# First tile of an attention kernel with two gated layers: low part of a weight unit issued inside the gate, first state pair split before the softmax

## The chip, the cores and the metric

The kernel runs on one core of one Trainium2 chip. The metric is the device time of one execution in microseconds (us), the median of three runs. The engines are TensorE (PE in the profile: matrix products; PEld: its weight loads), VectorE (DVE), ScalarE (ACT), GpSimd (POOL) and SyncE (SP). Each engine works through its own instructions in program order and waits at the head of its queue for semaphores. DMAs are issued from the queues of SP, ACT and POOL.

## The reference

```python
B, H, S, Ns, D = 8, 8, 512, 32, 64
scores  = x @ state.T / sqrt(D);  a  = softmax(scores)    # per batch and head
xread   = a @ state                                        # 512 rows per batch
scores2 = state @ x.T / sqrt(D);  a2 = softmax(scores2)
sread   = a2 @ x                                           # 32 rows per batch
x = concat(xread, sread) -> [4352, 512]                    # 8 * (512 + 32) tokens
h = x @ w_in1;  x = (h * sigmoid(1.702 * h)) @ w_out1      # 512 -> 2048 -> 512
h = x @ w_in2;  out = (h * cos(h)) @ w_out2
```

The weights arrive as 64-bit floating-point numbers, all else as float32.

## The kernel before

**Precision.** Every matrix product of the two layers is made of three products of halves: each operand is split into a high part (rounded to fp32r by a ScalarE copy) and a low part (VectorE: the value minus its high part), and high by high, high by low and low by high are summed in PSUM.

**Weights.** One layer's weights are cut into 16 units of 1 MB, named i0 to i7 (input side) and o0 to o7 (output side); a unit serves two chunks of 128 hidden features. Units are fetched in the order i0, i1, o0, i2, o1, i3, o2, ..., i7, o6, o7 (`seq`). The 64-bit words are decoded in the first tile's steps, each unit in five passes of 128x1024 elements. `decode_begin` (line 107) makes two ScalarE passes, `top` (line 120, into one of two buffers `u`) and `bottom` (line 123, in place on the raw words); `decode_end` (line 127) makes `bits` (VectorE, line 136, joins the two), `hi` (ScalarE, line 142) and `lo` (VectorE, line 146). A unit is begun in one step and ended in the next.

**Steps.** Tokens are worked in 9 tiles (8 batches of 512 rows and a tail of 256 rows), the hidden features in 16 chunks. The main loop (line 612) has one step for each layer m, tile t and chunk c. A step issues, in this order: `hidden` (chunk c of h, 12 products of 512 columns for the first tile), `second` of the chunk two steps back (12 products into the four `py` accumulators; its results free that chunk's `gh` and `gl`), the `gate` of chunk c, DMA fetches, `split_state` or `load_pair` where due, attention pieces of the next batch (`run_piece`), `sw_piece`s, and last the `lo()` that `gate` returned.

`gate` (line 376) issues on ScalarE: tanh (382), `top` of the next unit, `gh` (372), `bottom` of the next unit, `hi` of the unit begun a step earlier; and on VectorE: line 384 (the gate's product), `bits` (136), `gl` (374). In step c of the first tile the unit ended is seq[c + 1]: in odd steps c = 1, 3, ..., 13 it is o0 to o6, first needed by `second` in step c + 1, behind step c + 1's `hidden`; in even steps it is an input unit, first needed by `hidden` of step c + 2 (for i1, step 2).

**Attention in the first tile.** The pieces of batch 1 run in tile 0: the first halves of the heads in steps 1 to 8, the second halves in steps 8 to 15. On VectorE the larger ones are `max_n` and `max_s` (steps 2 and 9), `norm_s` (4, 11), `norm_n` (5, 11), `place_s` (9, 15). Their PSUM tiles (`psA`, `psB`, `psC`) come from a pool of two buffers, `psa`.

**State times input weights.** For tiles 1 to 7 the input product is folded: `sw_piece` (line 167) multiplies the split states of a pair of batches (`rhi`, `rlo`) by the input weights into a `psS` tile, from the same pool `psa`; ScalarE copies its high part (179), VectorE makes the low part (180), and GpSimd issues its store to DRAM (183). Pair 0's pieces are issued in steps 2, 4, 5, 6, 7, 7, 10, 11, 11, 12, 13, 13 and 15 of tile 0 and the next ones in tile 1. The tables `sw_steps` and `todo_split` (lines 516 and 526) set these steps by hand: pair 0 is split in step 1 of tile 0, pair 1 in step 7 of tile 1, and three steps after a split the next pair is loaded into the same `rblk`.

**Prologue.** Lines 557 to 598: batch 0's attention on the token side, with unit i0 decoded between its passes. The state of batch 0 is loaded into `rblk` from ScalarE's queue, used by `xread`, and then `load_pair(0)` follows into the same buffer from SP's queue. The whole schedule is written by hand (`manual_schedule`).

Of the kernel before, what the change touches and what calls it, by code (L numbers as in the profile page):

```python
# [10 lines left out]
F32 = mybir.dt.float32  # L11
# [3 lines left out]
AF = mybir.ActivationFunctionType  # L15
ALU = mybir.AluOpType
# [4 lines left out]
B, H, S, NS, D = 8, 8, 512, 32, 64  # L21
DM, DFF = 512, 2048
P = 128
KD = DM // P
# [17 lines left out]
def attention_two_mlps(  # L42
# [12 lines left out]
    nc = tc.nc  # L55
# [6 lines left out]
    op = ctx.enter_context(tc.tile_pool(name="op", bufs=2))  # L62
# [7 lines left out]
    PAIRS = ((1, 2), (3, 4), (5, 6), (7,))  # L70
# [8 lines left out]
    rblk = const.tile([P, KD, P], F32, name="rblk")  # L79
    rhi = const.tile([P, KD, P], F32R, name="rhi")  # L80
    rlo = const.tile([P, KD, P], F32R, name="rlo")
# [8 lines left out]
    def fetch_w(m, nm, j):  # L90

        src = {"i": (w_in1, w_in2), "o": (w_out1, w_out2)}[nm][m]
        raw = wp.tile([P, UNIT, 2], I32, name=f"raw{nm}{m}_{j}", tag=f"w{nm}{j}")
        for e in range(2):
            words = src[2 * j + e].bitcast(I32)
            if nm == "i":
                nc.sync.dma_start(
                    out=raw.rearrange("p (k e f) w -> p k e (f w)", k=KD, e=2)[:, :, e, :],
                    in_=words.rearrange("p (k f) -> p k f", k=KD),
                )  # L100
            else:
                nc.sync.dma_start(out=raw.rearrange("p (e d) w -> p e (d w)", e=2)[:, e, :], in_=words)
        rawt[m, nm, j] = raw
# [91 lines left out]
    at = ctx.enter_context(tc.tile_pool(name="at", bufs=1))  # L195
# [6 lines left out]
    def load_state(b, queue=nc.sync):  # L202
        queue.dma_start(out=rblk.rearrange("p k d -> p (k d)"), in_=st[b])

    def load_pair(p):

        for i in range(2):
            nc.sync.dma_start(
                out=rblk[:, :, i * D:(i + 1) * D], in_=stT[(*PAIRS[p], 0)[i]].rearrange("p (k c) -> p k c", k=KD)
            )  # L210

    def split_state():
        nc.scalar.activation(out=rhi, in_=rblk, func=AF.Copy)
        nc.vector.tensor_tensor(out=rlo, in0=rblk, in1=rhi.bitcast(F32), op=ALU.subtract)

    def load_xT(b, g, tags=("xT0", "xT1")):
        for j in range(2):
# [158 lines left out]
    def gate(t, c, stores, unit):  # L376

        bits, hi, lo = decode_end()
        top, bottom = decode_begin(*unit) if unit else (lambda: None,) * 2
        ph = ht.pop((0, t, c))  # L380
        t1 = ep.tile([P, sizes[t]], F32, name="t1", tag="t1")
        nc.scalar.activation(out=t1, in_=ph, func=AF.Tanh, scale=0.5 * GATE)  # L382
        g = t1
        nc.vector.scalar_tensor_tensor(out=g, in0=t1, scalar=1.0, in1=ph, op0=ALU.add, op1=ALU.mult)  # L384
        bits()
        for s in stores[:1]:
            s()
        if not stores:
            top()
        low = split_g(0, t, c, g)  # L390
        for s in stores[1:]:
            s()
        if stores:
            top()
        bottom()
        hi()
        low()
        return lo

    def cosine(t, c, stores, before, unit, end):  # L400

# [89 lines left out]
    def warm(n):  # L491

        ps = ps_y.tile([P, P], F32, name="idle", tag="py3")
        for _ in range(n):
            nc.tensor.matmul(ps, ident, ident, start=True, stop=True)
# [30 lines left out]
    todo_split = {step: p for p, (step, _) in enumerate(sw_steps)}  # L526
# [28 lines left out]
    with tc.manual_schedule():  # L555
        seq = [("i", 0), ("i", 1)] + [(nm, j + 2 * (nm == "i")) for j in range(KF // 2) for nm in "oi" if nm == "o" or j + 2 < KF // 2]
        load_xT(0, 0)
        load_state_t(0, nc.scalar)
        load_xT(0, 1, ("a20", "a21"))
        load_state(0, nc.scalar)  # L560
        fetch_w(0, *seq[0])
        make_identity(nc, ident)
        nc.vector.memset(half_pi, math.pi / 2.0)
        first = [
            attn_pieces(0, 0, ((ps_h, "ph"), (ps_h, "ph"))),
            attn_pieces(0, 1, ((ps_y, "py0"), (ps_y, "py1")), "a2T", "a21"),
        ]
        new_x(("x", 0), S)
        warm(3)
        first[0]["scores"]()  # L570
        first[1]["scores"]()
        fetch_w(0, *seq[1])
        load_xT(1, 0)
        load_state_t(1)
        for u in seq[2:5]:
            fetch_w(0, *u)

        def do(*names):
            for name in names:
                first[int(name[-1])][name[:-2]]()  # L580

        do("max_n 0", "exp_n 0")
        for part in decode_begin(0, *seq[0]):
            part()
        do("max_n 1", "exp_n 1", "sum_n 0", "turn_n 0")
        warm(22)
        load_xN(1, 0)
        do("xread 0")
        bits, hi, lo = decode_end()
        bits()  # L590
        hi()
        do("sum_n 1", "turn_n 1", "split_x 0")
        lo()
        do("xread 1")
        load_pair(0)
        for part in decode_begin(0, *seq[1]):
            part()
        do("split_x 1")

        steps1 = [(0, t, c) for t in (*range(B - 1), B, B - 1) for c in range(KF)]  # L600
        steps2 = [(1, t, c) for t in (*range(B // 2), B, *range(B // 2, B)) for c in range(KF)]
        steps = steps1 + steps2
        order = [t for _, t, c in steps if c == 0]


        fetches = {(0, 0, c): (0, *u) for c, u in enumerate(seq[5:])}
        units = {(0, 0, c): (0, *u) for c, u in enumerate(seq[2:])}
        fetches.update({steps1[steps1.index((0, B, 0)) + 2 * j + 2]: (1, "i", j) for j in range(KF // 2)})
        fetches.update({steps[steps.index((0, B - 1, 0)) + 2 * j + 3]: (1, "o", j) for j in range(KF // 2)})
        at2 = [(0, B, c) for c in (6, 9, 12, 15)] + [(0, B - 1, c) for c in range(2, KF, 2)] + [(1, 0, c) for c in (3, 5, 7, 10, 12)]  # L610
        units.update({at_: (1, nm, j) for at_, (nm, j) in zip(at2, ((nm, j) for nm in "io" for j in range(KF // 2)))})
        for i, (m, t, c) in enumerate(steps):
            if m == 0 and c == 0 and t + 1 < B:
                new_x(("a", t + 1), S, range(2))
                plan(i, t)
            if i + 1 < len(steps):
                hidden(m, t, c)
            if i + 2 == len(steps):
                hidden(*steps[-1])
            stores = second(*steps[i - LAG]) if i >= LAG else []  # L620
            unit = units.get((m, t, c))
            if m == 0:
                lo = gate(t, c, stores, unit)
            else:
                lo = cosine(t, c, stores, steps[i - 1][1:] if steps[i - 1][0] == 1 else None, unit, i + 1 == len(steps))
            if (m, t, c) in fetches:
                fetch_w(*fetches[m, t, c])
            if m == 0 and (t, c) in todo_split:
                split_state()
            if m == 0 and (t, c - 3) in todo_split and todo_split[t, c - 3] + 1 < len(PAIRS):  # L630
                load_pair(todo_split[t, c - 3] + 1)
            for b, name in todo.pop(i, ()):
                run_piece(b, int(name[-1]), name[:-2])
            for piece in todo_sw.get((t, c), ()) if m == 0 else ():
                sw_piece(*piece)
            lo()
            if m == 0:
                if t == 0 and c in (9, 11, 13, 14):
                    load_sw(1, (c - 8) // 2)
                if t == 0 and c == KF - 1:  # L640
                    for j in range(4, 8):
                        load_sw(1, j)
                if t == 1 and c < 4 or 1 < t < B and c + 8 < KF:
                    load_sw(t, c + 8)
                if t == 1 and 7 <= c < 11:
                    load_sw(t, c + 5)
                if 0 < t < B - 1 and c >= 8:
                    load_sw(t + 1, c - 8)
            if m == 0 and t == B - 2 and c == KF - 2:
                split_tail()  # L650
            j = i // KF
            if j + 1 < len(order) and i + KF >= len(steps1):
                if c == 2:
                    load_y(order[j + 1])
                if c in (7, 9, 11, 13):
                    split_y(order[j + 1], (c - 7) // 2, nc.gpsimd if m else nc.vector)
        times(*steps[-1][1:])()
        for s in steps[len(steps) - LAG:]:
            for w in second(*s):
                w()  # L660
# [43 lines left out]
```

## Time and profile before

| what | value |
|---|---|
| median of three runs (lowest, highest) | 1492.33 us (1488.96, 1492.51) |
| the profiled execution's own time | 1492.88 us |
| its span | 1491.1 us |
| TensorE busy in the span | 1455.3 us, 98% |
| VectorE, ScalarE, GpSimd busy | 927.7, 646.7, 111.4 us |
| mean granted clock of TensorE | 0.994 |

The span is what the profiler covers; the execution's own time is 1.8 us longer. A busy engine is one that has an instruction under way; TensorE's products are pipelined, so that a product of 512 columns lasts 0.39 us in a row while one starts every 0.23 us. In a row of the timeline the first number is the start, the second the length, and the bracket at the end says how long the engine had been idle before it and what released it. The name `py` is the second product's accumulator, `ph` the hidden one's, `wo` and `wi` are units, `swo` a folded piece.

### The profile page before, as it was taken

How to read it: one execution, taken by the hardware profiler on the slowest of the kernel's cores; microseconds unless marked ns; L12 is line 12 of the kernel's file. 1: busy time of each engine (PE TensorE's matmuls, PEld its weight loads, DVE VectorE, ACT ScalarE, POOL GpSimd, SP SyncE). 2: the span in 40 equal slices, each digit the busy share in tenths (PEclk: the TensorE clock that was granted, in tenths of full speed). 3: DMA queues.
4: the chain of work that ended last, by engine and by line, in shares of the span. 5: the costliest groups of instructions: out<-in, count | busy, mean ns of one | idle time of the engine just before them, and what ended most of it. 6: DMA issues, size and time to landing. Idle time of an engine off the chain costs nothing.

```text
span 1491.1 us, 19321 instructions
## 1 busy us (share of the span) xinstructions
PE 1455.3 (98%) x7306; PEld 1192.2 (80%) x7306; DVE 927.7 (62%) x1642; ACT 646.7 (43%) x1078; POOL 111.4 (7%) x155
## 2 busy tenths in 40 slices
PE   7979999999999999999999999999999999999998
PEld 4767778788888888898887888888888888888886
DVE  6765565556464646456678666666677666666665
ACT  5754434343434343466655333333344333333433
POOL 0111011101111000100001010000000000101000
PEclk9999999999999999999999999999999999999999
DMA  9655566565656453466400101000011001010000
GB/s 346 204 152 152 159 171 171 156 172 138 169 144 165 107 145 91 124 195 205 136 34 1 57 1 57 0 14 30 0 58 43 0 10 48 0 57 1 29 1 29
DMA packets 81340, 140.58 MB, mean 94 GB/s; under 512 B 11616, under 2 KB 38368, under 8 KB 81248
## 3 DMA queue, kind: packets, MB, share of 16 engines
q1 hardware_dynamic: 72000, 109.60, 23.4%
q0 software_dynamic: 8960, 29.37, 8.1%
q8 instruction: 57, 0.93, 0.3%
q10 hardware_dynamic: 288, 0.39, 0.1%
q14 instruction: 35, 0.29, 0.1%
HBM read 92.14 MB, written 47.19 MB: 93 GB/s over the span
## 4 chain that ended last, share of the span: by engine, by line
PE 81%; DVE 7%; ACT 3%; DMA 1%; issue 1%; POOL 0%; ACTq 0%; DVEq 0%
PE py L450 43%; PE ph L365 23%; PE ph L358 10%; PE psS L175 2%; PE psC L318 1%; DMA out<-o 1%; PE psA L234 1%; DVE r L411 1%; DVE r L416 1%; DVE d L415 1%; DVE gl L374 1%; DVE wo L146 1%; ACT gh L372 0%; ACT o L457 0%; DVE u L136 0%
## 5 line engine op out<-in xcount | busy, mean ns | idle before, releaser
L365 PE MATMUL ph<-xh,wi 128*128 128x512 f32 (+1 forms) x1280 | 404.0, 379 | 0.6 <-ACT wi L142 0.5
L450 PE MATMUL py<-gh,wo 128*128 128x512 f32 (+1 forms) x1152 | 367.0, 382 | 14.7 <-DVE wo L146 12.7
L450 PE MATMUL py<-wo,gh 128*128 128x512 f32 x1088 | 336.4, 390 | 1.0 <-ACT gh L372 0.7
L365 PEld LDWEIGHTS ph<-xh,wi 128*128 128x128 f32 x1280 | 237.2, 188 | 49.4 <-ACT wi L142 1.4
L450 PEld LDWEIGHTS py<-gh,wo 128*128 128x128 f32 x1152 | 215.0, 190 | 59.9 <-DVE wo L146 15.7
L365 PE MATMUL ph<-xl,wi 128*128 128x512 f32 (+1 forms) x640 | 241.0, 379 | 0.0
L450 PEld LDWEIGHTS py<-wo,gh 128*128 128x128 f32 x1088 | 202.8, 188 | 44.1 <-ACT o L457 2.3
L450 PE MATMUL py<-gl,wo 128*128 128x512 f32 (+1 forms) x576 | 219.1, 380 | 0.0
L450 PE MATMUL py<-wo,gl 128*128 128x512 f32 x544 | 213.0, 391 | 4.8 <-DVE gl L374 4.5
L374 DVE TENSOR_TENSOR gl<-t,gh 128x512 fp32r<-128x512 f32 (+1 forms) x144 | 97.4, 677 | 177.7 <-ACT gh L372 177.5
L418 ACT ACTIVATE r<-r,half_pi 128x512 f32<-128x512 f32 (+1 forms) x144 | 101.0, 701 | 245.5 <-DVE r L417 245.5
L372 ACT ACTIVATE gh<-t 128x512 fp32r<-128x512 f32 (+1 forms) x144 | 87.5, 608 | 256.8 <-PE py L450 160.3
L411 DVE TENSOR_SCALAR r<-r 128x512 f32<-128x512 f32 (+1 forms) x144 | 65.5, 455 | 180.2 <-ACT r L407 179.8
L358 PE MATMUL ph<-xh,swt 128*128 128x512 f32 x448 | 160.8, 399 | 0.0
L407 ACT ACTIVATE r<-ph 128x512 f32<-128x512 f32 (+1 forms) x144 | 82.3, 572 | 169.3 <-PE ph L365 169.3
L384 DVE SCALAR_TENSOR_TENSOR t<-t,ph 128x512 f32<-128x512 f32 (+1 forms) x144 | 94.1, 653 | 85.0 <-ACT t L382 84.7
L365 PEld LDWEIGHTS ph<-xl,wi 128*128 128x128 f32 x640 | 120.3, 188 | 22.9 <-DVE xl L286 0.2
L450 PEld LDWEIGHTS py<-wo,gl 128*128 128x128 f32 x544 | 102.1, 188 | 30.5 <-DVE gl L374 9.5
L450 PEld LDWEIGHTS py<-gl,wo 128*128 128x128 f32 x576 | 109.4, 190 | 20.4
L431 DVE TENSOR_TENSOR r<-r,ph 128x512 f32<-128x512 f32 (+1 forms) x144 | 94.6, 657 | 46.4 <-ACT r L418 46.4
L382 ACT ACTIVATE t<-ph 128x512 f32<-128x512 f32 (+1 forms) x144 | 82.0, 570 | 87.1 <-PE ph L358 68.7
L358 PEld LDWEIGHTS ph<-xh,swt 128*128 128x128 f32 x448 | 84.8, 189 | 28.5 <-issue 11.9
(76 smaller groups left out, 1490.6 us busy)
## 6 DMA issues: line engine op xcount, KB each, us to landing
sd<-swo POOLq DMA_DIRECT2D x112, 256.0 KB, 3.6
swt<-sd SPq DMA_DIRECT2D x112, 256.0 KB, 4.0
rawi<-in_w_in SPq DMA_DIRECT2D x32, 512.0 KB, 6.9
rawo<-in_w_out SPq DMA_DIRECT2D x32, 512.0 KB, 6.0
xT_t<-in_xT SPq DMA_DIRECT2D x36, 256.0 KB, 4.2
xN_t<-in_xN SPq DMA_DIRECT2D x16, 512.0 KB, 3.7
yd<-o SPq DMA_DIRECT2D x32, 256.0 KB, 3.3
yraw<-yd SPq DMA_DIRECT2D x32, 256.0 KB, 4.4
```

What stands on the lines that cost most here:

```text
L175: nc.tensor.matmul(out_, l[:, k, :], r[:, sl], start=(e == 0 and i == 0), stop=(e == 1 and i == 2), skip_group_check=True)
L358: nc.tensor.matmul(ph, l, r, start=(g == 0 and i == 0), stop=(g == 1 and i == 2))
L365: nc.tensor.matmul(ph, w[:, f0:f0 + P], x, start=(w is wh and k == 0 and x is xk[0][0]), stop=(w is wl and k == KD - 1))
L372: nc.scalar.activation(out=gh, in_=g, func=AF.Copy)
L374: return lambda: nc.vector.tensor_tensor(out=gl, in0=g, in1=gh.bitcast(F32), op=ALU.subtract)
L382: nc.scalar.activation(out=t1, in_=ph, func=AF.Tanh, scale=0.5 * GATE)
L384: nc.vector.scalar_tensor_tensor(out=g, in0=t1, scalar=1.0, in1=ph, op0=ALU.add, op1=ALU.mult)
L407: nc.scalar.activation(out=r, in_=ph, func=AF.Copy, scale=1.0 / (2.0 * math.pi), bias=0.25)
L411: nc.vector.tensor_scalar(out=r, in0=r, scalar1=MAGIC, scalar2=MAGIC, op0=ALU.add, op1=ALU.subtract)
L418: nc.scalar.activation(out=r, in_=r, func=AF.Sin, bias=half_pi)
L431: nc.vector.tensor_tensor(out=r, in0=r, in1=ph, op=ALU.mult)
L450: nc.tensor.matmul(yt[k], l, r, start=(c == 0 and i == 0), stop=(c == KF - 1 and i == 2))
```

## The change

In `gate`, `hi` is issued before `bottom` on ScalarE, and `lo` is issued at once behind `gl` on VectorE instead of at the end of the step; `gate` then returns an empty function. This holds for every gate of the first layer that ends a unit; `cosine` is as before. The first state pair is loaded in the prologue from ScalarE's queue into a buffer of its own (`pair0`, in the place of tag `xN`) and split ahead of the softmax, its low part on GpSimd; the split in step 1 and the load in step 4 go, and the load that stood behind `xread` brings pair 1. Two more warm-up products are issued before the scores.

```diff
-    def load_pair(p):
+    def load_pair(p, into=rblk, queue=nc.sync):
         for i in range(2):
-            nc.sync.dma_start(
-                out=rblk[:, :, i * D:(i + 1) * D], in_=stT[...]
+            queue.dma_start(
+                out=into[:, :, i * D:(i + 1) * D], in_=stT[...]
             )
-    def split_state():
-        nc.scalar.activation(out=rhi, in_=rblk, func=AF.Copy)
-        nc.vector.tensor_tensor(out=rlo, in0=rblk, in1=rhi.bitcast(F32), op=ALU.subtract)
+    def split_state(src=rblk, engine=nc.vector):
+        nc.scalar.activation(out=rhi, in_=src, func=AF.Copy)
+        engine.tensor_tensor(out=rlo, in0=src, in1=rhi.bitcast(F32), op=ALU.subtract)
...
+        hi()
         bottom()
-        hi()
         low()
-        return lo
+        lo()
+        return lambda: None
...
         load_state(0, nc.scalar)
+        pair0 = at.tile([P, KD, P], F32, name="pair0", tag="xN")
+        load_pair(0, pair0, nc.scalar)
         fetch_w(0, *seq[0])
...
-        warm(3)
+        warm(5)
...
+        split_state(pair0, nc.gpsimd)
         do("max_n 0", "exp_n 0")
...
-        load_pair(0)
+        load_pair(1)
...
-            if m == 0 and (t, c) in todo_split:
+            if m == 0 and todo_split.get((t, c), 0):
                 split_state()
-            if m == 0 and (t, c - 3) in todo_split and todo_split[t, c - 3] + 1 < len(PAIRS):
+            if m == 0 and todo_split.get((t, c - 3), 0) and todo_split[t, c - 3] + 1 < len(PAIRS):
                 load_pair(todo_split[t, c - 3] + 1)
```

## Rows read from the trace of the kernel before

**Rows 1.** The page, part 1: busy us, share of the span, instructions of TensorE.
```profile
PE 1455.3 (98%) x7306; PEld 1192.2 (80%) x7306; DVE 927.7 (62%) x1642; ACT 646.7 (43%) x1078; POOL 111.4 (7%) x155
```

**Rows 2.** Waits of TensorE, 0 to 140 us: us in total, times, longest.
```profile
PE py L450 <- DVE wo L146: 12.7, 7, 3.4
```

**Rows 3.** Windows of 12 us: length; busy us of PE, PEld, DVE, ACT, POOL; PEclk; DMA; GB/s.
```profile
28.00:40.00 12.00, 8.78 (x34) 6.65 (x33) 7.18 (x9) 7.74 (x11) 0.00 (x0) 0.86 1.06 377
88.00:100.00 12.00, 8.84 (x34) 6.65 (x33) 8.51 (x18) 5.72 (x7) 0.00 (x0) 0.86 0.49 169
108.00:120.00 12.00, 8.55 (x31) 6.78 (x30) 6.45 (x10) 5.49 (x9) 2.39 (x4) 0.72 0.36 89
```

**Rows 4.** Timeline around steps 1 and 2, several engines: start, length, instruction.
```profile
29.95 1.05 ACT L142 ACTIVATE wo<-u 128x1024 fp32r<-128x1024 f32 x1
...
31.06 0.50 PE L450 MATMUL py<-gh,wo 128*128 128x512 f32 x1 [1.57 <-ACT wo L142]
...
31.56 0.69 DVE L214 TENSOR_TENSOR rlo<-rblk,rhi 128x512 fp32r<-128x512 f32 x1 [1.78 <-ACT rhi L213]
32.17 1.22 DVE L146 TENSOR_TENSOR wo<-u,wo 128x1024 fp32r<-128x1024 f32 x1
...
33.44 1.22 PE L450 MATMUL py<-gh,wo 128*128 128x512 f32 x2 [1.65 <-DVE wo L146]
...
37.44 0.63 ACT L372 ACTIVATE gh<-t 128x512 fp32r<-128x512 f32 x1 [2.80 <-PE py L450]
```

**Rows 5.** Timeline of step 11 and the start of step 12.
```profile
103.91 0.68 DVE L384 SCALAR_TENSOR_TENSOR t<-t,ph 128x512 f32<-128x512 f32 x1
...
104.50 1.22 DVE L136 SCALAR_TENSOR_TENSOR u<-u,rawo 128x1024 int32<-128x1024 int32 x1
...
105.64 1.13 ACT L123 ACTIVATE rawi<-rawi 128x1024 int32<-128x1024 uint32 x1
...
106.39 0.15 DVE L301 TENSOR_SCALAR s<-s 128x1 f32<-128x1 f32 x1
...
106.67 1.06 ACT L142 ACTIVATE wo<-u 128x1024 fp32r<-128x1024 f32 x1
...
109.75 1.25 DVE L180 TENSOR_TENSOR swo<-psS,swo 128x512 fp32r<-128x512 f32 x2
...
110.92 1.20 DVE L146 TENSOR_TENSOR wo<-u,wo 128x1024 fp32r<-128x1024 f32 x1
...
112.18 1.22 PE L450 MATMUL py<-gh,wo 128*128 128x512 f32 x2 [3.45 <-DVE wo L146]
```

**Rows 6.** Timeline of VectorE in step 9.
```profile
88.50 1.79 DVE L329 STREAM_TRANSPOSE xs<-psC 32x32 f32<-32x32 f32 x8
...
92.51 1.22 DVE L146 TENSOR_TENSOR wo<-u,wo 128x1024 fp32r<-128x1024 f32 x1
```

**Rows 7.** Timeline of TensorE, second product of step 13 to that of step 14.
```profile
121.33 0.39 PE L450 MATMUL py<-gh,wo 128*128 128x512 f32 x1
...
124.05 0.40 PE L175 MATMUL psS<-wi,rhi 128*128 128x256 f32 x2
...
129.86 0.74 PE L450 MATMUL py<-gh,wo 128*128 128x512 f32 x2 [1.02 <-DVE wo L146]
...
132.39 0.86 PE L318 MATMUL psC<-xN_t,a2T 128*32 128x128 f32 x24
```

**Rows 8.** Timeline of the prologue, several engines.
```profile
9.44 0.63 ACT L249 ACTIVATE T<-T 128x512 f32<-128x512 f32 x1 [6.49 <-DVE T L248]
...
10.90 1.05 POOL L248 TENSOR_TENSOR T<-T,m 128x512 f32<-128x512 f32 x1 [9.59 <-DVE m L244]
...
11.38 0.59 DVE L259 TENSOR_SCALAR s<-s 128x16 f32<-128x16 f32 x1
...
15.47 0.17 DVE L259 TENSOR_SCALAR s<-s 128x16 f32<-128x16 f32 x1
```

**Rows 9.** Line 208, the pair's loads: us from issue to landing.
```profile
DMA to landing us min/median/max: 3.3/5.5/9.9
```

More of the change, by code (lines that the diff above doesn't have):

```diff
@@ L203, in load_state @@
         queue.dma_start(out=rblk.rearrange("p k d -> p (k d)"), in_=st[b])
-    def load_pair(p):
+    def load_pair(p, into=rblk, queue=nc.sync):
         for i in range(2):
-            nc.sync.dma_start(
-                out=rblk[:, :, i * D:(i + 1) * D], in_=stT[(*PAIRS[p], 0)[i]].rearrange("p (k c) -> p k c", k=KD)
-            )
-    def split_state():
-        nc.scalar.activation(out=rhi, in_=rblk, func=AF.Copy)
-        nc.vector.tensor_tensor(out=rlo, in0=rblk, in1=rhi.bitcast(F32), op=ALU.subtract)
+            queue.dma_start(
+                out=into[:, :, i * D:(i + 1) * D], in_=stT[(*PAIRS[p], 0)[i]].rearrange("p (k c) -> p k c", k=KD)
+            )
+    def split_state(src=rblk, engine=nc.vector):
+        nc.scalar.activation(out=rhi, in_=src, func=AF.Copy)
+        engine.tensor_tensor(out=rlo, in0=src, in1=rhi.bitcast(F32), op=ALU.subtract)
     def load_xT(b, g, tags=("xT0", "xT1")):
```

## The prediction

> **What bounds the kernel now.** The page comes first: TensorE is busy 98% of the span [rows 1], so 36 us of the span lie between its products, and an edit of the order can win only idle time and time at the lower clock. The table of who waited for whom says where: from 0 to 140 us TensorE waits seven times, 12.7 us in total, for VectorE's low part of an output unit (line 146) [rows 2]. These are the odd steps 1, 3, ..., 13 of the first tile, each ending an output unit that `second` needs one step later. The windows show a second price: three waits have the granted clock at 0.86, 0.86 and 0.72 of 2.4 GHz over 12 us [rows 3], part of the time at 1.2 GHz. The timeline shows both in one place: the unit's high part ends at 31.0, TensorE has by then waited 1.57; VectorE then splits the state pair, and the low part, released late, holds TensorE again for 1.65; the ten products left take from 33.44 to the next `gh` at 37.44, 4.0 us [rows 4], where ten after a short wait take 2.53 at full clock [rows 7]. Step 11 shows the usual pattern: VectorE does attention's norms from 106.39, two `swo` passes from 109.75, and only then the low part (110.92), although the high part had ended at 107.7; TensorE stands until 112.18 [rows 5].
>
> **The change part by part.** I call E(c) the end of `second` in step c; `gh` of step c waits for it, because two `gh` buffers stand against a lag of two.
>
> *The new order in the gate.* VectorE's passes follow each other at some 0.6 us (gate product, `gl`), 1.2 (`bits`) and 1.15 (`lo`), read from start to start [rows 5]; on ScalarE `gh` takes some 0.55, `bottom` 1.03, `hi` 0.95 [rows 4, 5]. Where nothing else is late, `gh` runs from E to E + 0.6, `hi` to E + 1.6 instead of E + 2.6, `lo` to E + 2.75. TensorE needs it behind `hidden` and two products, E + 2.72 + 0.46 = E + 3.2 (the 12 products of `second` take 2.72, 121.33 to 124.05 [rows 7], and those of `hidden` are alike). So an odd step closes its wait with 0.4 us to spare, and with a folded piece in it (0.73, half of 124.05 to 125.5) with 1.1. `bottom` moves 0.95 later, but ends where `hi` used to; the next `bits` stands behind tanh and the gate product, which hide it. `lo` comes earlier than the next `top` needs the buffer `u`, so ScalarE's waits for it go too.
>
> *What is then late.* Attention's passes and the `swo` passes stand 1.15 us later on VectorE than the same queue had them, plus up to 0.35 in which `lo` waits for `hi`. Two things hang on them: the next gate product, and the two `psa` buffers. I worked the steps through with the durations above. Steps 4 to 8 hold (VectorE at most 6.65 us against 6.7 of TensorE in step 5). Step 9 has 4.0 us of attention [rows 6], so VectorE needs 3.5 + 4.0 = 7.5 against 5.44 and passes 2 us on; counted from E(9): `lo` of step 9 to 2.7, attention to 6.75, `bits` of step 10 to 8.55, its `hi` and `lo` to 10.7; then `exp` on ScalarE and the copy and `swo` to 13.1; gate product and `bits` of step 11 to 14.8, `hi` to 15.8, `lo` to 17.0. TensorE has E(10) = 5.45, E(11) = 11.6; its second folded piece of step 11 waits 0.8 for a `psa` buffer (the `swo` at 13.1), `second` needs the low part at 16.95, a wait of 0.1, E(12) = 19.3. Step 11 has norms of 3.36 and two `swo` of 1.17 [rows 5]: they end at 21.5, and the transposes of step 12 wait 1.65 for the buffer that the first releases. With 0.2 in step 3 that leaves 2.8 us of waits beyond step 1.
>
> *Step 1.* The high part ends at 29.9 instead of 31.0, and the split of the state (0.61 on VectorE, 31.56 to 32.17) is gone; `lo` runs from 30.0 to 31.2, so the product that started at 33.44 starts at 31.25: 2.2 us. The earlier start of `hidden` in step 2 (i1's high part also comes before `bottom`) only lengthens the wait before it.
>
> *Prologue.* Two more DMA issues on ScalarE end some 6 us before its first pass at 9.44 [rows 8]. The pair must land before 8.8, or the copy to `rhi` holds the softmax. Issued by about 3 (an estimate: ScalarE's queue has two issues before it), it lands between 6.3 and 12.9 by the extremes of its present loads, 8.4 by their median [rows 9]; I take the median, which is the nearest kind of transfer: no delay; at the late end 3.9 us. Its 256 KB push other loads by 0.7 at 377 GB/s [rows 3]; the softmax's chain takes up to half of that, 0.3. The low part on GpSimd costs what line 248 costs there, 1.05 [rows 8], off the chain; but a VectorE pass of 16 elements that takes 0.17 took 0.59 beside it and ended with it [rows 8], so I put 0.4 for one such meeting, between 0 and 1.05. Sum 0.7, from 0 to 5.
>
> By the Trainium skill, "SBUF — State Buffer", section "SBUF: two separate sides", a GpSimd pass and a VectorE pass that needs the pair of ports they share do not split it: whoever starts first holds it throughout and the other stands still. The row of 0.59 agrees. By it the next two-input VectorE pass could wait the whole GpSimd pass, and the sum would be 0.65 us smaller; by the row it is as taken.
>
> By the Trainium skill, "DMA: Bandwidth & Descriptors", section "Queues, rings and completion order", each DMA engine takes turns between the queues that have work. By it the pair, alone in ScalarE's queue, lands near the early end and the sum stands; by the late end of rows 9 (from SP's queue, behind others) it would be 3.9 smaller.
>
> *The rest.* The warm-up products run while TensorE has no operands for the scores: nothing, or their own length if the state came sooner. The load that went from step 4 shortens SP's queue; the pair-1 load takes its old place. Gates of the later tiles that end units have no attention between `gl` and `lo`: zero.
>
> **The sum**, against the profiled execution's 1492.88. Step 1: 2.2 of wait, and 1.4 of slow clock (4.0 less 2.53) if the shorter waits (1.25 and 0.8 by my times) keep the clock. The other six places: 12.7 - 1.65 = 11.05, less the 2.8 left: 8.25. Slow clock after the two longest waits: the windows lose 12 x 0.14 = 1.7 and 12 x 0.28 = 3.4; a wait of 3.2 to 3.45 lies in each, so I take 4.0 of the 5.1. Restarts: ten products take 2.53 instead of 10 x 0.227, six places against four: 0.5. Less the prologue's 0.7: 2.2 + 1.4 + 8.25 + 4.0 + 0.5 - 0.7 = 15.65; my step-by-step times give 0.5 more, since the folded piece of step 12 also ran at the low clock: 16.2. 1492.9 - 16.2 = 1476.7; the median of the runs is 0.55 under the profiled one: 1476.
>
> **The rivals.**
> *The wait changes its name (psa bound).* VectorE's total in steps 9 to 12 is only reordered: 7.5 + 4.7 + 8.0 us. If the folded pieces and transposes wait for `swo` about as long as `second` did for `lo`, the two deep places keep 6.6 us and their 4.0 of clock: 16.2 - 10 = 6, about 1486.5. For it: step 11's 4.5 us of other passes. Against: TensorE has `second` (2.72) to do meanwhile.
> *Slower: every folded piece waits.* `lo` ahead of `swo` delays each release by 1.15 + 0.35 = 1.5. If no piece has slack, 12 pieces in steps 2 to 13 cost 18, more than 16.2, and with the prologue's late end 3.9 the time is 1492.3 - 16.2 + 18 + 3.9 = 1498. It decides from 11 pieces on. Against: my times leave 0.9 to 2.1 us between a buffer's release and its next use in steps 5, 7 and 13.
> *The pair lands late.* Forecast plus 3.9: 1480; inside the range.
> *No effect.* If `hi` is late on ScalarE anyway, because `bits` ends after `gh`, `lo` waits for it in the gate and TensorE as long as before: 1490 to 1493. For it: in step 11 `bits` ended at 105.7, as `gh` did [rows 5]. Against: `hi` still starts 1.03 earlier, and in step 11 3.2 us passed between its end and `lo`.
>
> **How the numbers follow.** Forecast (late pair included) 0.80, renamed wait 0.11, no effect 0.05, slower 0.04. All waits, all slow clock and the restarts gone would be 12.7 + 1.6 + 6.8 + 0.5 = 21.6 us: 1471, with the rounding 1470; the renamed wait reaches 1486.5, and I close the range at 1484. A change under 0.3% (4.5 us) can't be told from none here. Faster takes the first case and the renamed wait, 0.91, within 0.3% 0.05, slower 0.04.
>
> **What would show it.** Right: no waits of `py` for line 146 beyond 1 us after step 1; granted clock 1.0 from 88 to 110; `hi` directly behind `gh`; state reads of step 14, at 132.4 [rows 7], about 16 us earlier; small waits of `psS` and `psB` for `swo` in steps 11 and 12. Wrong: the first `exp` after 10.5 (late pair), waits of `psS` in most steps (slower rival), or `lo` standing long for `hi` (no effect).

## The result and the profile after

The changed kernel takes 1477.41 us (1474.31 to 1477.99, four runs) against 1492.36 beside it, a ratio of 0.9902 (95% interval 0.9890 to 0.9914). Run once more beside the later experiments it gave 0.9893 (0.9877 to 0.9908). The forecast was 1476, range 1470 to 1484, and faster.

Part 1 of the page and TensorE's waits from 0 to 140 us of the changed kernel (us in total, times, longest):

```profile
PE 1450.5 (98%) x7310; PEld 1190.5 (81%) x7310; DVE 927.4 (63%) x1641; ACT 646.8 (44%) x1078; POOL 112.7 (8%) x156
```

```profile
PE psX L280 <- DVE aT L266: 3.4, 2, 2.5
...
PE psB L309 <- DVE swo L180: 1.3, 1, 1.3
PE py L451 <- ACT wo L142: 1.1, 1, 1.1
PE psS L175 <- DVE swo L180: 1.1, 1, 1.1
PE py L451 <- DVE wo L146: 1.0, 2, 0.5
```

Of the 12.7 us of [rows 2] 1.0 is left (the lines below the gate have moved by one), and two small waits have come for the `swo` passes. The windows of [rows 3] read:

```profile
28.00:40.00 12.00, 10.26 (x48) 6.67 (x47) 8.79 (x11) 9.84 (x12) 0.00 (x0) 1.00 1.03 370
88.00:100.00 12.00, 10.93 (x56) 9.01 (x56) 9.54 (x14) 7.58 (x12) 1.19 (x2) 1.00 0.33 109
108.00:120.00 12.00, 12.00 (x88) 9.98 (x86) 9.49 (x13) 9.56 (x14) 3.59 (x6) 1.00 0.56 131
```

The clock is 1.00 in all three. The places of [rows 4] and [rows 5], in the timeline (start, length, instruction):

```profile
33.99 1.23 DVE L146 TENSOR_TENSOR wo<-u,wo 128x1024 fp32r<-128x1024 f32 x1 [0.58 <-ACT wo L142]
34.02 0.50 PE L451 MATMUL py<-gh,wo 128*128 128x512 f32 x1 [1.15 <-ACT wo L142]
...
35.27 0.73 PE L451 MATMUL py<-gh,wo 128*128 128x512 f32 x2 [0.53 <-DVE wo L146]
...
97.21 0.51 PE L175 MATMUL psS<-wi,rhi 128*128 128x256 f32 x2 [1.07 <-DVE swo L180]
...
100.07 1.23 DVE L146 TENSOR_TENSOR wo<-u,wo 128x1024 fp32r<-128x1024 f32 x1 [0.59 <-ACT wo L142]
101.22 0.14 DVE L301 TENSOR_SCALAR s<-s 128x1 f32<-128x1 f32 x1
...
104.56 1.25 DVE L180 TENSOR_TENSOR swo<-psS,swo 128x512 fp32r<-128x512 f32 x2
...
105.27 0.66 PE L309 MATMUL psB<-ident,a 128*128 128x128 f32 x4 [1.32 <-DVE swo L180]
...
119.14 1.08 PE L318 MATMUL psC<-xN_t,a2T 128*32 128x128 f32 x32
```

The low part (100.07) stands ahead of the norms (101.22) and the `swo` passes (104.56), and `second` no longer waits for it there; the transposes of step 12 wait 1.32 instead. The state reads of step 14 start at 119.14, 13.25 earlier than in [rows 7].

The prologue went the other way. Timeline of ScalarE and TensorE before, then of ScalarE, GpSimd, VectorE and TensorE in the changed kernel:

```profile
1.66 1.28 ACT L249 ACT_TABLE_LOAD   x1 [1.66 <-PEq L693]
...
17.46 1.13 PE L280 MATMUL psX<-aT,rblk 64*128 64x512 f32 x4 [2.24 <-DVE aT L266]
18.52 0.50 PE L365 MATMUL ph<-xh,wi 128*128 128x512 f32 x1
...
21.96 0.60 ACT L382 ACTIVATE t<-ph 128x512 f32<-128x512 f32 x1 [2.03 <-PE ph L365]
```

```profile
9.74 1.28 ACT L213 ACT_TABLE_LOAD   x1 [9.74 <-DMA pair<-in_stT]
...
11.03 0.63 ACT L213 ACTIVATE rhi<-pair 128x512 fp32r<-128x512 f32 x1
11.57 0.61 ACT L249 ACTIVATE T<-T 128x512 f32<-128x512 f32 x1
...
12.98 1.06 POOL L248 TENSOR_TENSOR T<-T,m 128x512 f32<-128x512 f32 x1
...
13.43 1.15 DVE L262 TENSOR_TENSOR T<-T,r 128x512 f32<-128x512 f32 x1
...
19.06 2.08 PE L280 MATMUL psX<-aT,rblk 64*128 64x512 f32 x4 [2.54 <-DVE aT L266]
21.07 0.79 PE L365 MATMUL ph<-xh,wi 128*128 128x512 f32 x1
...
25.84 0.60 ACT L382 ACTIVATE t<-ph 128x512 f32<-128x512 f32 x1 [3.58 <-PE ph L365]
```

ScalarE stands until 9.74 for the pair, then loads its activation table, then splits, and the first `exp` comes at 11.57 instead of 9.44 [rows 8]. The four products of the second read of `x` (`psX`) last 2.08 instead of 1.13, and a product of step 0's `hidden` 0.79 instead of 0.50: TensorE is at the lower clock there (granted clock 0.50 from 18 to 24 us, 1.00 before). The first tanh is at 25.84, against 21.96 before.

### The profile page after: what moved, and what is told of

Its sections match the earlier page's. It is cut to its first block, busy times and chain, and to the rows that moved or that the text cites. A ratio compares the mean times of both kernels' runs of the same rounds, so it can differ in the third digit from the quotient of the medians.

```text
span 1475.6 us, 19334 instructions
## 1 busy us (share of the span) xinstructions
PE 1450.5 (98%) x7310; PEld 1190.5 (81%) x7310; DVE 927.4 (63%) x1641; ACT 646.8 (44%) x1078; POOL 112.7 (8%) x156
## 4 chain that ended last, share of the span: by engine, by line
PE 86%; DVE 8%; ACT 3%; issue 1%; DMA 1%; POOL 0%; ACTq 0%; DVEq 0%
PE py L451 45%; PE ph L365 25%; PE ph L358 10%; PE psS L175 3%; PE psC L318 1%; PE psA L234 1%; DVE u L136 1%; DVE r L412 1%; DVE r L417 1%; DVE d L416 1%; DVE wo L146 1%; DVE gl L374 1%; ACT wo L142 1%; DMA pair<-in_stT 0%; PE psB L309 0%
## 5 line engine op out<-in xcount | busy, mean ns | idle before, releaser
L451 PE MATMUL py<-gh,wo 128*128 128x512 f32 (+1 forms) x1152 | 363.3, 379 | 2.4 <-ACT wo L142 1.1
```

What stands on the lines that cost most here:

```text
L451: nc.tensor.matmul(yt[k], l, r, start=(c == 0 and i == 0), stop=(c == KF - 1 and i == 2))
```

## The experiments

Two landmarks of the profiled execution of each kernel separate the prologue from the first tile: the first tanh (step 0) and the first `psC` product of step 14. Times in us; the clock is TensorE's granted clock from 14 to 26 us, where the prologue ends; the ratio is to the kernel before, run beside it.

| kernel | clock, 14 to 26 | first tanh | step 14 | between | rest of the span | ratio (95% interval) |
|---|---|---|---|---|---|---|
| before | 1.00 | 21.96 | 132.39 | 110.43 | 1358.7 | |
| changed | 0.72 | 25.84 | 119.14 | 93.30 | 1356.5 | 0.9902 (0.9890 to 0.9914) |
| changed, again | 0.86 | 23.90 | 117.22 | 93.32 | 1356.6 | 0.9893 (0.9877 to 0.9908) |
| gate alone | 1.00 | 21.81 | 115.11 | 93.30 | 1357.7 | 0.9894 (0.9880 to 0.9907) |
| pair alone | 1.00 | 21.95 | 129.78 | 107.83 | 1355.4 | 0.9983 (0.9974 to 0.9992) |
| pair alone, again | 0.86 | 23.84 | 127.90 | 104.06 | 1355.8 | one run |
| split late | 1.00 | 22.87 | 116.21 | 93.34 | 1356.2 | 0.9892 (0.9879 to 0.9906) |
| table early | 1.00 | 22.21 | 115.53 | 93.32 | 1356.3 | 0.9881 (0.9868 to 0.9895) |
| pair all late | 1.00 | 25.09 | 118.50 | 93.41 | 1356.7 | 0.9903 (0.9888 to 0.9918) |
| `hi` first alone | 0.86 | 23.18 | 131.68 | 108.50 | 1355.5 | 1.0005 (0.9995 to 1.0016) |
| `lo` first alone | 1.00 | 21.95 | 121.50 | 99.55 | 1357.7 | 0.9934 (0.9921 to 0.9947) |
| gate, pieces first | 1.00 | 23.12 | 117.07 | 93.95 | 1347.4 | 0.9830 (0.9817 to 0.9844) |
| gate, `lo` twice | 1.00 | 24.47 | 131.64 | 107.17 | 1362.3 | 1.0027 (1.0018 to 1.0036) |
| changed, table early, pieces first | 1.00 | 21.87 | 115.73 | 93.86 | 1349.9 | 0.9842 (0.9829 to 0.9855) |

**The gate alone.** The kernel before with the gate's two edits.

```diff
+        hi()
         bottom()
-        hi()
         low()
-        return lo
+        lo()
+        return lambda: None
```

> The kernel before with the gate's new order alone (hi ahead of bottom, lo issued in the gate); the state pair is loaded and split as before. Theory G (the gate's order is the whole gain, the early split costs 3.9 us in the prologue): prologue as before, hidden of step 0 starts at 18.5; the two products of step 1 to 2 gain about 3.5, steps 2 to 14 gain 13.5: 1473.5 to 1476, faster than the changed kernel. Rival S (the split's removal from step 1 is what saves step 1 and its clock): waits of step 2 stay near 3 us, 1478 to 1480.

Measured: 1476.04, 93.30 between the landmarks, the same to 0.02 as the changed kernel, with the split still in step 1. Theory G holds for the first tile: the gate's order is the whole gain. Its second half, faster than the changed kernel, is not shown: the intervals of the two overlap. Rival S falls: step 2 waits 1.16 and 0.53, as in the changed kernel.

**The pair alone.** The changed kernel with the old order in the gate (the diff above reversed).

> The changed kernel with the old order in the gate: early load and split of pair 0, lo at the end of the step. Theory G: prologue 3.9 us longer, 0.6 to 2 won back in step 1, the seven waits for line 146 stay at 11 to 13 us: 1493.5 to 1496, slower than before. Rival S: 1489 to 1491.

Measured: 1488.46, faster than before: both forecasts missed. In this execution the pair landed at 8.15 and the first tanh was on time:

```profile
8.15 1.28 ACT L213 ACT_TABLE_LOAD   x1 [8.15 <-DMA pair<-in_stT]
9.44 0.63 ACT L213 ACTIVATE rhi<-pair 128x512 fp32r<-128x512 f32 x1
9.98 0.61 ACT L249 ACTIVATE T<-T 128x512 f32<-128x512 f32 x1
...
21.95 0.60 ACT L382 ACTIVATE t<-ph 128x512 f32<-128x512 f32 x1 [2.04 <-PE ph L365]
```

So the prologue does not always lose 3.9. Under the old order the split's going from step 1 wins 2.6 to the step-14 landmark: 0.9 in waits (13.9 us of `second` and `hidden` from 15 to 140 us, 14.8 before), the rest at the clock of step 1 (1.00 from 28 to 40 us, 0.86 before). Beside the new order it wins nothing.

**The split late.** The pair's DMAs as in the changed kernel, its split at the end of the prologue.

```diff
-        split_state(pair0, nc.gpsimd)
         do("max_n 0", "exp_n 0")
...
-        load_xN(1, 0)
         do("xread 0")
...
         do("split_x 1")
+        split_state(pair0, nc.gpsimd)
+        load_xN(1, 0)
```

> The changed kernel with the split of pair 0 moved from ahead of the softmax to the end of the prologue, the load of xN(1,0) behind it; the pair's DMAs stay where they are. Theory P (ScalarE stands at the head of its queue for the pair until 9.7 us, and the activation table's load of 1.28 comes only then): first exp back at about 9.4 to 10, hidden of step 0 at 18.5 to 19, clock kept: 1473 to 1474.5. Rival Q (the pair's DMAs delay the tiles of x and unit i0, the split merely waits beside it): first exp stays over 11, no more than 1 us gained, 1476.5 to 1477.5.

Measured: 1475.53. The first `exp` is back at 9.17, as theory P said, but the first `top` then waits 2.48 us for unit i0 (12.28), as rival Q said; the first tanh comes at 22.87. Each is half right.

**The table early.** The changed kernel with one small Exp at the start.

```diff
         nc.vector.memset(half_pi, math.pi / 2.0)
+        early = sm.tile([P, 1], F32, name="early", tag="m2")
+        nc.scalar.activation(out=early, in_=half_pi, func=AF.Exp)
```

> The changed kernel with one Exp of 128x1 elements (on half_pi, result unused) at the start of ScalarE's queue, so that its activation table is loaded at about 3 us. Theory P: of the delay of the first exp (11.57 against 9.44) 1.28 goes, first exp at about 10.3; 1.3 us gained, up to 2.8 if TensorE's idle time before step 0 then stays short enough for the full clock: 1474.5 to 1476. Rival Q: first exp unchanged, since other loads are late: 1477 to 1477.5.

Measured: 1474.05. The table is loaded at 2.99, the split at 8.69, the first `exp` at 9.22, the first tanh at 22.21. Its interval overlaps the changed kernel's, so the gain is seen in the trace and not settled by the times.

**The pair's loads and split both late.** As "split late", with the pair's DMAs issued behind the second `exp`.

```diff
-        load_pair(0, pair0, nc.scalar)
...
         do("max_n 1", "exp_n 1", "sum_n 0", "turn_n 0")
+        load_pair(0, pair0, nc.scalar)
```

> The changed kernel with the pair's two DMAs issued from ScalarE's queue behind the second exp (about 13 us) and its split at the end of the prologue. Theory Q' (what the pair costs in the prologue is its DMAs: while they stand in ScalarE's queue, SyncE issues unit i0's fetch at 4.1 to 4.3 instead of 2.6, and i0 lands later; the head-of-line wait of ScalarE comes on top): the fetch is issued at 2.6 again, the first top does not wait, hidden of step 0 starts at 18.4 to 18.7, the state reads of step 14 at 115.5 to 116.5: 1.5 to 3 us under the changed kernel run beside it, within 1.5 us of the gate alone. Rival P (ScalarE's wait alone): the same as with only the split late, first top still waits for its unit.

Measured: 1475.82, a miss. Unit i0's fetch is issued at 2.60 again, and still its first `top` waits until 11.91; theory Q' is wrong about that cause. And the pair, issued at 13.35 and 15.52, lands only at 24.55, with ScalarE standing for it:

```profile
13.35 0.61 ACTq L208 DMA_DIRECT2D pair<-in_stT  x1
...
15.52 0.55 ACTq L208 DMA_DIRECT2D pair<-in_stT  x1
...
24.55 0.63 ACT L213 ACTIVATE rhi<-pair 128x512 fp32r<-128x512 f32 x1 [3.36 <-DMA pair<-in_stT]
25.09 0.58 ACT L382 ACTIVATE t<-ph 128x512 f32<-128x512 f32 x1
```

Nor does a late i0 need the pair: "gate, pieces first" (first `top` at 11.56) and "gate, `lo` twice" (12.08) wait for it with the old loads. In the six kernels that keep the prologue of the kernel before, the first `top` stands between 9.87 and 12.08: when i0 lands differs by some 2 us, for a reason that stays open.

**The gate's halves.** The kernel before with `hi` ahead of `bottom` and nothing else, and the kernel before with `lo` issued in the gate and `hi` left behind `bottom`.

```diff
+        hi()
         bottom()
-        hi()
```

> The kernel before with hi ahead of bottom alone; lo stays at the end of the step. Theory L (VectorE's queue order holds lo back): only the places where lo waited for hi gain (step 3, step 1's high part), 0.5 to 2 us in all, waits for line 146 stay at 10 to 12.5 us: 0.9985 to 1.0 of before. Rival H (the earlier hi is what lets second start): a third or more of the 15 us: below 0.9965.

```diff
-        return lo
+        lo()
+        return lambda: None
```

> The kernel before with lo issued in the gate behind gl alone; hi stays behind bottom. Theory L: lo waits for hi about 1 us longer on VectorE, so that steps without a folded piece keep waits of 0.5 to 1 us and the queue of steps 9 to 12 grows by about 2: most of the gain, 11 to 14 us, 0.9905 to 0.9925 of before, waits for line 146 of 2 to 5 us. Rival H: less than half of the gain, above 0.995.

`hi` alone gives nothing (1491.51). Its shorter time between the landmarks (108.50) is not the order's: the waits are as long as before (15.2 us, 14.8 before), and the granted clock from 88 to 100 us happens to be 1.00 instead of 0.86. TensorE's waits, 15 to 140 us, first of that kernel, then of the one with `lo` alone (1480.54):

```profile
PE py L450 <- DVE wo L146: 14.0, 7, 3.5
...
PE py L450 <- ACT wo L142: 1.2, 1, 1.2
```

```profile
PE py L451 <- ACT wo L142: 2.7, 2, 1.6
...
PE py L451 <- DVE wo L146: 2.0, 4, 0.5
PE psS L175 <- DVE swo L180: 1.6, 1, 1.6
PE psB L309 <- DVE swo L180: 1.4, 1, 1.4
```

Theory L holds in kind: VectorE's order held `lo` back. `lo` alone gives 10.9 of the 17.1 us between the landmarks, less than the 11 to 14 expected of the whole time; with `lo` moved, the earlier `hi` is worth the other 6.2. Of these, 3.6 are waits (8.2 us with `lo` alone, 4.6 with the gate alone), and up to 1.7 are the clock from 28 to 40 us (0.86 against 1.00).

**The pair alone, again.** The same kernel as "the pair alone".

> A second look at the early pair with the old gate order (same kernel as the run with the pair alone), for the spread of the pair's landing: so far 8.15, 8.69 and 9.74 us. Theory Q': the landing moves by a microsecond or more from one execution to the next, and hidden of step 0 starts at 18.5 where it lands before about 9, over 20 where it lands after 9.5. If the landing is at 8.1 to 8.2 again, the spread belongs to the kernels and not to the executions.

The pair landed at 8.82, 0.67 later than in the first trace (Q' had a microsecond or more), its split started at 10.12 behind the table load, and `hidden` of step 0 at 19.19 instead of 18.52. The first tanh came at 23.84: the same program loses 1.9 us in one execution and none in another. Only 0.67 of that is the landing; the other 1.2 lie in that `hidden`, at the lower clock (0.86 from 14 to 26 us).

Behind the prologue the two traces of this one program differ more. The waits for line 146 are alike (11.7 and 12.2 us, the longest 3.6 in both), but the clock is not. Windows of the first trace, then of the second:

```profile
88.00:100.00 12.00, 8.84 (x35) 7.22 (x35) 6.34 (x10) 5.74 (x10) 0.00 (x0) 0.86 0.30 121
108.00:120.00 12.00, 10.23 (x38) 8.49 (x39) 6.25 (x8) 5.87 (x8) 2.71 (x5) 0.72 0.36 89
```

```profile
88.00:100.00 12.00, 8.83 (x41) 6.82 (x40) 7.91 (x17) 7.20 (x12) 0.00 (x0) 1.00 0.50 179
108.00:120.00 12.00, 9.88 (x52) 8.45 (x53) 8.32 (x11) 6.95 (x10) 3.59 (x6) 1.00 0.44 105
```

The second is 3.8 shorter between the landmarks (104.06 against 107.83) with waits no shorter: waits of 3.6 us brought the lower clock in one execution and not in the other.

**The pieces first.** The gate alone, and the folded pieces issued ahead of attention's.

```diff
-            for b, name in todo.pop(i, ()):
-                run_piece(b, int(name[-1]), name[:-2])
             for piece in todo_sw.get((t, c), ()) if m == 0 else ():
                 sw_piece(*piece)
+            for b, name in todo.pop(i, ()):
+                run_piece(b, int(name[-1]), name[:-2])
```

> The gate's order alone, and in every step the folded pieces issued ahead of attention's pieces (on TensorE, ScalarE and VectorE). Theory B (the waits left after the change, 1.1 for psS and 1.3 for psB, come from swo standing behind attention's passes on VectorE): both go, the state reads of step 14 move from 116.25 to about 114; the two waits of psS for swo in later tiles (4.2 us) may go too: 2 to 6 us under the gate alone, 1470 to 1474 or 0.986 to 0.988 of before. Rival A (VectorE's total in steps 9 to 12 is the bound, whatever the order): the waits come back under other names, within 1 us of the gate alone.

Measured: 1466.21, the fastest kernel of the study. But not where theory B said first: between the landmarks it is 93.95, no better than 93.30, and waits of 0.9 (`psS`), 0.4 and 0.5 stand where 1.1 and 1.3 stood. In the first tile rival A is right. The gain is behind it, 1347.4 against 1357.7. TensorE's waits from 118 to 700 us, the gate alone and then this kernel:

```profile
PE psS L175 <- DVE swo L180: 4.2, 2, 2.4
```

```profile
PE psS L175 <- DVE swo L180: 0.4, 1, 0.4
```

7.9 of the 10.3 us lie ahead of the second layer (from the `psC` of step 14 to its first `Sin`: 593.8 against 601.7). Of these, 3.8 are the waits shown and up to 1.8 the clock behind the first of them (0.94 from 190 to 220 us in the gate alone, 1.00 here); 2.3 stay open. The rest of the 10.3 lies in the second layer, which this edit does not touch.

**The low part twice.** The gate alone with the same pass issued twice.

```diff
         low()
         lo()
+        lo()
         return lambda: None
```

> The gate's order alone, with the low part computed twice in each gate (the second pass writes the same values): 1.15 us more of VectorE in each of the steps 0 to 14. Theory B (each psa buffer has 0.9 to 2.1 us of slack in steps 2 to 7 and 13, so that only steps 9 to 12 pay): waits of psS and psB grow from 2.4 to 6 or 8 us and waits of step 1 by nothing, 4 to 7 us slower than the gate alone. Rival W (every folded piece waits as soon as VectorE's passes stand later): 12 pieces by 1.15, 12 to 15 us slower, about the kernel before.

Measured: 1495.09, slower than before; the first tile loses 13.9. That is rival W's size, but not its way: `psS` and `psB` wait 3.9 in all, and `second` waits 7.7 in six places, because the second pass writes what it reads. The run shows that the low part has less than 1.15 to spare in most odd steps; it does not measure the slack of `psa`.

**The changed kernel again, and with both additions.** The second is the changed kernel with the table early and the pieces first (both diffs above).

> The changed kernel itself once more, beside the next one, for its prologue in another execution. If the loss of 3.9 us at the first tanh (25.84 against 21.96) belongs to the kernel, the first tanh stands again at 25 or later and the ratio is 0.990 or more. If it hangs on when the pair and unit i0 land (seen: the pair at 8.2 to 10.1, i0's first pass at 9.9 to 12.3, the latter late also without the pair), the first tanh can stand anywhere from 22 to 26; the state reads of step 14 follow it by 94 to 95 us in either case.

> The changed kernel with its activation table loaded early (one small Exp) and the folded pieces ahead of attention's in every step. Theory: the early pair is worth nothing beside the new gate order (0.6 less than the gate alone at step 14 in the runs so far), so the same as gate and pieces without it: 0.982 to 0.984 of before, 1465 to 1468. Rival: the split's removal from step 1 does count here (2.6 us, as it did under the old gate order): 0.980 to 0.982, 1462 to 1465.

The changed kernel's first tanh was at 23.90 this time (pair landed at 8.89, split at 10.18), 93.32 from there to step 14: the size of the loss differs between executions, and was not zero in either trace. Both additions together give 1467.80, 0.9842: no better than gate and pieces without the pair, as the theory said.

## Why the prediction was right

*The first tile.* The forecast's terms without the prologue sum to 16.2 + 0.7 = 16.9 us; between the landmarks the change wins 110.43 - 93.30 = 17.13, and the gate's order alone wins the same. Step by step: the waits of step 2, forecast 1.25 and 0.8, are 1.15 and 0.53; the product forecast 2.2 earlier is 2.05 earlier against the first tanh (35.27 - 25.84 against 33.44 - 21.96); the clock kept its full level there; the piece of step 11 waits 1.07 (forecast 0.8), the transposes of step 12 1.32 (1.65). VectorE's queue in steps 9 to 12 came out as worked: the low part of step 11 ends 17.6 after E(9) (forecast 17.0).

Of the 17.13, 10.3 are waits of `second` and `hidden` (14.8 us before, 4.5 after; forecast 10.45) and the other 6.8 the clock and the restarts (forecast 6.4). The clock part is right in size and less sure than the forecast took it: all eight traces with both halves of the new order, `lo` twice aside, have the full clock from 28 us to step 14, but the second trace of the pair alone kept it behind waits as long as those before. That each long wait costs clock is not shown; that this execution of the kernel before lost it there, and the changed kernel did not, is.

*The prologue was mis-sized.* Its term was 0.7, measured 3.88 in the first trace of the changed kernel and 1.94 in the second. Two steps failed. The first is the bound of 8.8 for the landing, and with it "no delay" for the first `exp`. The pair landed near the median that was taken (8.4): at 9.74 and 8.89 in the two traces, at 8.15 to 8.82 in the four others that show it. But the 1.28 of the activation table was not in the sum: before, it is loaded while ScalarE has nothing to do (1.66); now it stands behind the wait, and the pair would have had to land by some 7.6. With the table early, landings at 8.69 and 8.31 delayed nothing (first `exp` at 9.22 and 9.00). The forecast's own sign of a late pair, a first `exp` after 10.5, showed in both traces (11.57 and 10.72). In the first it is 2.13 late (9.74 + 1.28 + 0.55 = 11.57). VectorE takes back 0.58 of it, since its sum pass stood 1.23 behind that `exp` before and stands 0.65 behind it now; the second `psX` is 1.60 late (19.06 against 17.46).

The second failed step is the clock, for which the prologue's sum had no term. The other 2.28 of the 3.88 are TensorE at 1.2 GHz: 0.95 in those `psX` products, 1.33 in `hidden` of step 0, with a granted clock of 0.72 from 14 to 26 us, against 1.00 before. In the second trace it is 0.74 of lateness and 1.20 of clock (0.86). That the pair brings the lower clock is not shown: "`hi` first alone", with the old prologue and its first `exp` at 9.46, has 0.86 there too and its first tanh at 23.18. TensorE stood 2.54 us before the second `psX` in it, in both traces of the changed kernel and in the first of the pair alone, where the clock stayed at 1.00. What decides it stays open. I had listed a late pair as worth 3.9, for a landing at 12.9; that the loss had this size is a coincidence.

The 1.15 pass is a multiplication of two inputs beside a GpSimd subtraction. The Trainium skill, "SBUF — State Buffer", section "SBUF: two separate sides", has one of them stand still. The trace agrees: 0.61 of the pass lies beside GpSimd's, which runs from 12.98 to 14.04, and the 0.54 left after it (14.04 to 14.58) is most of the 0.69 that the pass takes undisturbed. The meeting costs the chain nothing new: before, the same GpSimd pass met a pass of 0.17, which took 0.59 [rows 8]. The 0.4 put down for a meeting with the pair's own GpSimd pass (11.75 to 13.04) came to nothing: the VectorE passes that start beside it, at 12.22 and 12.94, take 0.69 and 0.17. The other rule weighed, turns between DMA queues (the Trainium skill, "DMA: Bandwidth & Descriptors", section "Queues, rings and completion order"), would by the prediction have landed the pair near the early end, 6.3; the 7.1 us median from issue to landing in the changed kernel, against 4.2 for `rblk` from the same queue, does not bear that out.

*What made the total come close.* At step 14 the change is 13.25 ahead; the span ends 15.5 ahead. The remaining 2.2 arise in the second layer, whose order is the same in both programs: from step 14 to its first `Sin` (733.98 before, 720.92 after) it is 601.6 and 601.8 us, from there to the end 757.1 and 754.7. In the kernels that leave the parts behind step 14 alone (all rows but the three with the pieces first or `lo` twice) the rest of the span lies between 1355.4 and 1357.7, and 1358.7 before, so I count it as scatter between executions. It covered two thirds of the prologue's miss, and that is luck.

*The rivals.* The renamed wait came to 2.4 us, as in the forecast's own sum. "Every piece waits" and "no effect" did not occur.

## What to carry to other kernels

Where an engine's queue holds a short pass that the bottleneck waits for, behind passes that nobody waits for yet, issue it as soon as its input can be there, and move that input up with it: here the low part alone gave two thirds and the high part alone nothing. Before putting work that waits for a DMA at the head of a queue, look at what stood in the idle time there: a table load can end up behind the wait. Judge an edit that is bundled with another by itself; the early split was worth 2.6 us under the old order, and nothing under the new. And compare the granted clock of both traces before you put a difference down to the order: two executions of one program differed by 3.8 us with the same waits.

## What the runs showed of the hardware that I had not expected

With the pair's two DMAs in ScalarE's queue at the start, SyncE issued unit i0's fetch at 4.04 to 4.34 us in all seven traces; without them there, at 2.59 or 2.60 in all seven. The two are different queues, but the waits of SyncE (line 97 is the fetch) name what it stood for, before and in the changed kernel:

```profile
SPq L97 <- DMA sblk<-in_stT: 0.4, 1, 0.4
```

```profile
SPq L97 <- DMA sblk<-in_stT: 1.5, 1, 1.5
```

In both traces eight loads are issued, counted over the two queues, and the ninth waits until the first, `sblk`, has landed. Before, the ninth is the third weight fetch (4.29); with the pair's two loads ahead it is the first (4.11). So it is a wait that this program's loads have for each other, and not a meeting of the queues.

A transfer of 256 KB in pieces of 256 bytes, issued at 13.35 and 15.52 while the DMA engines were busy (share 0.94 from 14 to 26 us), landed 9 us after its last issue.
